# Splitting half of one 2 MB weight transfer by rows in a two-layer cached-attention decode

## The chip, the cores and the metric

The kernel runs on one core of a Trainium2 chip. The core has engines for computing (PE, the matrix engine; DVE, the vector engine; ACT, the scalar engine; POOL, GpSimd) and SP, SyncE, which here issues the transfers from HBM into the on-chip memory of 128 rows (SBUF). The transfers themselves are carried out by 16 DMA engines. The metric is device time in microseconds of one execution; lower is better.

## The reference

Two layers of the same pair of blocks, with the same weights and the same cache in both layers, run on one token for each of two sequences:

```python
x = x + A(layernorm(x), k_cache, v_cache, wq, wo)
x = x + B(layernorm(x), W_gate, W_up, W_down)
# and once more the same two lines
```

Block A is attention of one query position on a cache: 32 query heads of 128, in groups of 4 on 8 cached heads, 32768 cached positions, softmax over them, and the way out through `wo` (4096 x 512). Block B is a gated unit: `(gate * (gate > 0)) * up`, with `gate` and `up` of width 1792, and the way down to 512. All is float32. The cached keys and values are 8 x 2 x 32768 x 128 numbers each, 268 MB each in one layer's reading, so two layers read some 1.1 GB.

## The kernel before

**Tiling.** A pair of a cached head and a sequence is one turn; a layer has 16 turns (`NG`, L17). The keys of a turn are a matrix of 128 rows by 32768 numbers, and the values likewise. Each comes in two halves of 128 rows of 64 KB (8 MB), so a turn has four such transfers: first half of keys, second half of keys, first half of values, second half of values. They go into three buffers of 8 MB (`X`, `Z`, `Y`, L34) that are used in rotation. A transfer can start only when PE has finished with what the buffer held.

**A turn** (`lap`, L615 to L637) runs in this order: the second half of the values of the turn before (PE, into the accumulator `acc`); the keys' first half, among whose blocks the output of the turn before is multiplied with the way out's weights (`head_out`, `project`); the keys' second half; the softmax (DVE, ACT); the values' first half. Turns are a hardware loop on PE, DVE and ACT. SP isn't in the loop: its issues are written out one after the other, and it issues them in the order in which the program names the transfers. An issue that has to wait holds back all that stand behind it.

**The way out's weights.** `wo` is laid out as 128 rows; a cached head has 8 KB in each row (`WO`, L46). Two heads' shares lie side by side in a place of 16 KB a row (`WO_AT`). In layer 1 the heads run downward. At the end of each odd turn from turn 3 on either the next two heads' shares are loaded (`fetch_out`, L367, called at L635, in turns 3, 7 and 11), or POOL copies the second of them (`other`) to the place from which PE reads (`weights`), or, in the last turn, one head's share is loaded (L633). In layer 1 `weights` is the second 8 KB of a row and `other` the first. The next issue on SP after such a load is the second half of the same turn's values, at the start of the next turn; after it come the two halves of that next turn's keys. The first of these is given `(weights,)` as a further thing to wait for (L619), so that PE, which waits for the keys, needn't wait for the weights as well.

**Semaphores.** Each transfer has a lane, a semaphore that counts its completions. Transfers into the three buffers have a lane for each buffer; the loads of `wo` in the turns have the lane `wo`; all others go through 16 lanes in turn (`LANES`, L33; `fetch`, L353). A transfer on a lane waits for the one before it on the same lane.

**The end of layer 1** reads the last half of values in three pieces, then the gated unit's weights (`wgu`, three transfers, `UNITS`) and the way down (`wd`, six transfers, `DOWN`), all 128 rows high, and writes 64 KB out.

Of the kernel before, what the change touches and what calls it, by code (L numbers as in the profile page):

```python
# [11 lines left out]
P = 128  # L12
# [20 lines left out]
LANES = 16  # L33
# [11 lines left out]
P_AT, MT_AT, ACS_AT, WO_AT = FLOW, FLOW + 2 * D, FLOW + 2 * D + 32, FLOW + 3 * D + 32  # L45
WO = 4 * D  # L46
# [9 lines left out]

UNITS = (5, 3, 2, 1, 5, 2, 3, 4, 2, 3, 2), (16, 8, 8)
DOWN = (4, 3, 2, 4, 1), (4, 4, 2, 2, 1, 1)
QUERY = 4, 2, 3, 3, 1, 3, 2, 3, 2, 2, 3, 2, 2

C_SAME, C_SELH, C_PAIR, C_COL, C_HALF, C_MEAN, C_END = 0, 128, 144, 176, 178, 180, 181
# [247 lines left out]
def attention_reglu_decode(nc, hold, x, k, v, wq, wo, wgu, wd, out):  # L309
    tape = Tape(nc)  # L310
    pe, dve, act, pool, sp = map(tape.engine, ("tensor", "vector", "scalar", "gpsimd", "sync"))

    def sbuf(name, width):
        return hold.enter_context(nc.sbuf_tensor(name, [P, width], F32))[:, :]
# [4 lines left out]
    arena = sbuf("arena", ARENA)  # L319
# [9 lines left out]
    def tile(at, width):  # L329
        return arena[:, at : at + width]  # L330
# [8 lines left out]
    turn = [0, FLOW, 0, RING[0]]  # L339
# [8 lines left out]
    def ring(width):  # L348
        at = turn[1] if turn[1] + width <= RING[1] else turn[3]
        turn[1] = at + width  # L350
        return at

    def fetch(at, src, lane=None, also=()):  # L353
        t = arena[:, at : at + src.shape[-1]]
        if lane is None:
            lane = f"lane{turn[2] % LANES}"
            turn[2] += 1
        sp.dma_start(t, src, lane=lane, also=also)
        return t

    def half(src, n, h, at, also=()):
        return fetch(at, src[n, h], f"slot{at // ROW}", also)
# [4 lines left out]
    def fetch_out(h, n, t, lane="wo"):  # L367
        return fetch(t.offset, wo[:, h * WO : (h + n) * WO], lane)

    dve.memset(xq, 0.0)  # L370
    for b in range(NB):
        act.dma_start(bass.AP(xq.tensor, xq.offset + b * P, [[32 * P, 4], [1, P]]), x[:, b, :], lane=f"x{b}")
# [63 lines left out]
    def queries(L, total, first, between):  # L436
# [7 lines left out]
        else:  # L444
            begins = {sum(QUERY[:e]): n for e, n in enumerate(QUERY)}
        for e, b in enumerate(order):
# [29 lines left out]
    def place_queries(n, step=0):  # L476
        dve.tensor_copy(qz[:, 28 : 28 + REP], moving(lambda turn: bass.AP(
            qT.tensor, qT.offset + (1 + n) * REP + turn * (step * REP), [qT.ap[0], [1, REP]])))
# [8 lines left out]
    def soft_max(scores=scores):  # L487
        m1, nm, rs = own(0), own(1), own(2)
        dve.tensor_reduce(m1, scores, AX.XY, ALU.max)
        mt = tile(MT_AT, 32)  # L490
        dve.tensor_scalar_mul(mt, pair, m1)
        pe.matmul(small[0][:, :32], same, mt, start=True, stop=True)
        dve.tensor_reduce(nm, small[0][:, :32], AX.X, ALU.max, negate=True)
        act.activation(tile(P_AT, 2 * D), scores.rearrange("p a b -> p (a b)"), AF.Exp, bias=nm, scale=1.0, accum_out=rs)

    def soft_tail():
        pT, p = tile(PT_AT, 2 * D), tile(P_AT, 2 * D)
        for B in range(2):
            dve.transpose(pT[:, B * D : (B + 1) * D], p[:, B * D : (B + 1) * D])
        pe.matmul(small[1][:, 0:1], same, own(2), start=True, stop=True)  # L500
        dve.reciprocal(own(3), small[1][:, 0:1])
# [11 lines left out]
    def evacuate(split=True):  # L513
        acs = tile(PT_AT if split else ACS_AT, D)
        w = P if split else D
        for t in range(0, D, w):
            dve.tensor_scalar_mul(acs[:, t : t + w], acc[:, t : t + w], own(3))
        return acs

    def head_out(b, acs, weights=None):  # L520
        for t in range(4):
            pe.matmul(small[0][:, :REP], acs[:, t * P : (t + 1) * P], selh[:, 4 * t : 4 * t + 4], start=t == 0, stop=t == 3)
        if weights is not None:
            project(weights)
            dve.memset(oT, 0.0)
        dve.tensor_copy(moving(lambda turn: bass.AP(oT.tensor, oT.offset + (turn + b) % NB, [oT.ap[0], [NB, REP]])), small[0][:, :REP])
# [28 lines left out]
    def feed_forward(last, total):  # L555
# [25 lines left out]
        c = 0  # L581
        for n in DOWN[last]:
            t = fetch(Z + c * D if last else ring(n * D), wd[:, c * D : (c + n) * D])
# [11 lines left out]
    for L in range(NLAYER):  # L595
        last = L == NLAYER - 1
# [8 lines left out]
        def keys(h, t, first=0, scores=scores):  # L605
            for e in range(0, t.shape[-1] // D, 8):
                k_blocks(h + e, t[:, e * D : min(t.shape[-1], (e + 8) * D)], first, scores)
                yield e

        def values(lo, t, first=False, final=False):  # L610
            n = t.shape[-1] // D
            for e in range(0, n, 8):
                v_blocks(lo + e, lo + min(e + 8, n), t[:, e * D : min(e + 8, n) * D], first and e == 0, final and e + 8 >= n)

        def lap(i, second, k_first):  # L615

            values(HALF, second or half(v, seq[i - 1], 1, b), False, True)
            evacuate(False)
            for e in keys(0, k_first or half(k, seq[i], 0, a, (weights,) if i > L else ())):  # L619
                if e == 8:  # L620
                    head_out(1, tile(ACS_AT, D), weights)
            if not last and i == NG - 1:
                pool.tensor_copy(tile(RING[1], KEPT), tile(a, KEPT))
            for _ in keys(HALF, half(k, seq[i], 1, c)):
                pass
            soft_max()
            soft_tail()
            values(0, half(v, seq[i], 0, a), True)
            place_queries(seq[L] + step, step)
            if i % 2 == 1 and i > 1 and (last or i + 1 < NG):  # L630
                h = seq[i] // NB
                if h == 0:
                    fetch_out(h, 1, weights)  # L633
                elif i % 4 == 3:
                    fetch_out(h - last, 2, tile(WO_AT, 2 * WO))  # L635
                else:
                    pool.tensor_copy(weights, other)  # L637

# [7 lines left out]
        if last:  # L646
            n, e = divmod(KEPT, D)
# [28 lines left out]
        for i in tape.laps(range(L, NG), 1):  # L676
            lap(i, *ready.pop(i, (None, None)))
        nothing(op, False)
        combine()
        n = seq[NG - 1]  # L680
        for lo, hi in ENDING if last else FLOWN:
            t = fetch(b + lo * D, v[n, 1, :, lo * D : hi * D])
# [44 lines left out]
```

## Time and profile before

| | |
|---|---|
| time, median of 3 runs | 2556.66 us (2556.43 to 2556.95) |
| time of the profiled execution | 2556.44 us |
| its span, first to last instruction | 2555.0 us |
| PE busy | 1332.5 us (52%) |
| DVE, ACT, POOL busy | 156.9, 60.3, 18.2 us |
| read from HBM | 1102.99 MB, 432 GB/s over the span |

The page splits the span in 40 slices and gives for each the mean busy share of the 16 DMA engines and what they moved. Queues are told apart by number: q1 is the one that SP's transfers go through, q10 that of ACT's two small loads of x, and the queues of the kind "instruction" bring the program's code. A packet is one piece that a DMA engine moves; those of 4 bytes are completions. In the timeline an entry with SPq is the issue of a transfer, not the transfer. A wait at L212 is one of several waits ahead of an instruction, one at L214 the last, attached to the instruction itself.

### The profile page before, as it was taken

To read this page: it belongs to the slowest core of one execution; us is meant where nothing else is said; L and a number is where in the kernel's file an instruction comes from. 1 tells how busy PE (TensorE), PEld (TensorE's weight loads), DVE (VectorE), ACT (ScalarE), POOL (GpSimd) and SP (SyncE) were. 2 spreads that over 40 slices of the span, in tenths; PEclk is the share of its full clock that TensorE was granted. 3 is DMA by queue.
4 is the path that set the end of the run, shared out by engine and by line. 5 is a ranking of instruction groups with operands and counts; after the bars stand their busy time and mean duration, and the time that the engine had idled before them with its cause. 6 is when DMAs were issued, how large, how long until landed. Compare 5 with 4: busy or idle time off the path is not lost.

```text
span 2555.0 us, 20568 instructions
## 1 busy us (share of the span) xinstructions
PE 1332.5 (52%) x9542; PEld 364.7 (14%) x9542; DVE 156.9 (6%) x409; ACT 60.3 (2%) x82; POOL 18.2 (1%) x25
## 2 busy tenths in 40 slices
PE   4554545445444554455586554455445544454456
PEld 1111111111111111111121111111111111111112
DVE  1000000000000000000111000000000000000001
ACT  0000000000000000000000000000000000000000
POOL 0000000000000000000000000000000000000000
PEclk9777767777777777777798777777766777677778
DMA  9999999999999999999999999999999999999999
GB/s 425 429 440 427 428 442 430 440 429 434 434 430 440 430 433 434 430 440 430 424 422 440 431 439 429 434 434 433 437 429 435 434 433 436 429 437 432 434 435 391
DMA packets 26526, 1103.28 MB, mean 432 GB/s; under 512 B 2952, under 2 KB 3216, under 8 KB 6928
## 3 DMA queue, kind: packets, MB, share of 16 engines
q1 hardware_dynamic: 26496, 1103.06, 100.0%
q8 instruction: 12, 0.20, 0.0%
q14 instruction: 2, 0.02, 0.0%
q10 hardware_dynamic: 16, 0.00, 0.0%
HBM read 1102.99 MB, written 0.07 MB: 432 GB/s over the span
## 4 chain that ended last, share of the span: by engine, by line
DMA 73%; PE 26%; issue 0%; SPq 0%; DVE 0%; ACT 0%; ACTq 0%
DMA arena<-k 37%; DMA arena<-v 34%; PE acc L214 12%; PE pair L214 11%; DMA arena<-wd 1%; PE op L214 1%; PE small L214 1%; DMA arena<-wgu 1%; DMA arena<-wq 1%; SPq L214 0%; DVE pair L214 0%; DVE stat L214 0%; DVE arena L214 0%; DVE small L214 0%; DVE xq L214 0%
## 5 line engine op out<-in xcount | busy, mean ns | idle before, releaser
L214 PE MATMUL acc<-arena 128*16 128x512 f32 (+2 forms) x4288 | 616.3, 730 | 530.8 <-DMA arena<-v 521.5
L214 PE MATMUL pair<-arena,qz 128*32 128x512 f32 x4098 | 587.8, 727 | 558.9 <-DMA arena<-k 558.9
L214 PEld LDWEIGHTS pair<-arena,qz 128*32 128x32 f32 x4098 | 150.2, 131 | 987.1 <-issue 699.1
L214 PEld LDWEIGHTS acc<-arena 128*16 128x16 f32 (+1 forms) x4288 | 137.7, 113 | 972.5 <-issue 603.1
L214 ACT ACTIVATE arena<-pair,stat 128x1024 f32<-128x1024 f32 x32 | 35.6, 1113 | 2386.9 <-DVE stat L214 2386.9
L214 DVE TENSOR_SCALAR arena<-acc,stat 128x512 f32<-128x512 f32 (+1 forms) x39 | 25.5, 667 | 1052.1 <-PE acc L214 1052.1
L214 DVE TENSOR_REDUCE stat<-pair 128x1 f32<-128x1024 f32 x32 | 39.2, 1224 | 633.9 <-PE pair L214 633.9
L214 DVE STREAM_TRANSPOSE arena<-arena 128x512 f32<-128x512 f32 (+1 forms) x68 | 43.4, 674 | 40.8 <-ACT arena L214 40.7
L214 PE MATMUL small<-stat,cst 128*128 128x1 f32 (+1 forms) x72 | 16.2, 295 | 48.6 <-ACT arena L214 48.6
L214 PE MATMUL small<-arena,cst 128*128 128x32 f32 x64 | 13.1, 286 | 51.6 <-DVE arena L214 51.6
L214 PEld LDWEIGHTS small<-cst,arena 128*128 128x128 f32 x264 | 32.1, 191 | 28.9 <-issue 27.2
L214 PE MATMUL small<-cst,arena 128*128 128x4 f32 x264 | 35.0, 256 | 0.5 <-DVE arena L214 0.5
L214 PE MATMUL op<-arena,oT 128*2 128x512 f32 (+1 forms) x312 | 34.4, 526 | 0.4 <-DVE oT L214 0.3
L214 DVE MEMSET oT<- 128x8 f32 x33 | 2.1, 65 | 511.7 <-PE op L214 511.7
L214 POOL COPY arena<-arena 128x2048 f32<-128x2048 f32 (+1 forms) x7 | 13.4, 1921 | 2191.4 <-PE op L214 2045.7
L214 PE MATMUL op<-arena 128*32 128x448 f32 (+1 forms) x128 | 20.0, 572 | 5.6 <-DMA arena<-wq 3.1
L214 PEld LDWEIGHTS small<-stat,cst 128*128 128x128 f32 x72 | 13.2, 229 | 56.9 <-ACT arena L214 52.2
L214 PEld LDWEIGHTS small<-arena,cst 128*128 128x128 f32 x64 | 9.5, 188 | 80.5 <-DVE arena L214 80.5
L214 ACT ACT_TABLE_LOAD x16 | 20.5, 1283 | 11.4 <-DMA xq<-x 11.2
L214 PE MATMUL acc<-cst 128*32 128x448 f32 (+1 forms) x48 | 18.3, 479 | 0.0
L214 PE MATMUL small<-cst,stat 128*128 128x2 f32 x8 | 1.7, 287 | 18.7 <-DVE stat L214 18.1
L214 PE MATMUL small<-arena 128*32 128x128 f32 x224 | 8.8, 277 | 3.0 <-DMA arena<-wd 2.3
(63 smaller groups left out, 98.8 us busy)
## 6 DMA issues: line engine op xcount, KB each, us to landing
arena<-wo SPq DMA_DIRECT2D x6, 2048.0 KB, 32.0
arena<-v SPq DMA_DIRECT2D x2, 4096.0 KB, 37.8
arena<-wo SPq DMA_DIRECT2D x4, 1024.0 KB, 26.0
arena<-wd SPq DMA_DIRECT2D x4, 1024.0 KB, 23.4
arena<-wq SPq DMA_DIRECT2D x5, 768.0 KB, 6.3
arena<-wgu SPq DMA_DIRECT2D x1, 3584.0 KB, 44.1
arena<-wgu SPq DMA_DIRECT2D x2, 1792.0 KB, 48.4
arena<-v SPq DMA_DIRECT2D x2, 1536.0 KB, 40.9
```

Source lines behind the costliest of these rows:

```text
L214: ins = getattr(engine, op.call)(*args, **op.kw)
```

## The change

In turn 7 of layer 1 the load of two heads' shares (128 rows of 16 KB) is replaced by seven transfers. The first has all 128 rows of the first 8 KB (`other`). The second 8 KB (`weights`) come as six transfers of rows 0, 1, 2 to 3, 4 to 7, 8 to 31 and 32 to 127. All seven use the 16 lanes in turn rather than the lane `wo`. All other loads stay.

```diff
+FEW = (0, 1), (1, 2), (2, 4), (4, 8), (8, 32), (32, P)
...
+    def fetch_few(h, n, t):
+        fetch(t.offset, wo[:, h * WO : (h + n - 1) * WO])
+        for lo, hi in FEW:
+            at = t.offset + (n - 1) * WO
+            sp.dma_start(arena[lo:hi, at : at + WO], wo[lo:hi, (h + n - 1) * WO : (h + n) * WO], lane=f"lane{turn[2] % LANES}")
+            turn[2] += 1
...
-                    fetch_out(h - last, 2, tile(WO_AT, 2 * WO))
+                    (fetch_few if last and i == 7 else fetch_out)(h - last, 2, tile(WO_AT, 2 * WO))
```

## The prediction

> **What bounds the kernel now.** I read the page first (its transfers, its queues, the chain), then the stretches around the place of the change, the sync queue's waits there, and last the transfers' own view of the final 4 us.
>
> ```profile
> span 2555.0 us, 20568 instructions
> DMA packets 26526, 1103.28 MB, mean 432 GB/s; under 512 B 2952, under 2 KB 3216, under 8 KB 6928
> q1 hardware_dynamic: 26496, 1103.06, 100.0%
> q8 instruction: 12, 0.20, 0.0%
> q10 hardware_dynamic: 16, 0.00, 0.0%
> DMA 73%; PE 26%; issue 0%; SPq 0%; DVE 0%; ACT 0%; ACTq 0%
> ```
>
> SyncE's queue q1 fills 100.0% of the time of the 16 DMA engines. The chain gives 26% to PE, but that is a matter of how it hops: a landing, the matmuls that it frees, the buffer that they free, the next issue. It doesn't mean that the engines of the transfers rest meanwhile. The stretches of one turn in layer 1 say the same:
>
> ```profile
> core 0: us, PE busy (x) PEld busy (x) DVE busy (x) ACT busy (x) POOL busy (x), PEclk, DMA share, GB/s
> 1849.00:1887.00 38.00, 20.46 (x132) 5.36 (x132) 3.08 (x7) 1.21 (x2) 0.00 (x0) 0.69 1.01 435
> 1887.00:1912.00 25.00, 9.89 (x64) 2.03 (x64) 0.75 (x1) 0.00 (x0) 0.00 (x0) 0.66 1.00 435
> ```
>
> PE works 20.46 of 38 us, the transfers all of it. So the bytes are the bound: at 435 GB/s over 16 engines one engine moves 27.2 GB/s, and a row of 8 KB takes 8192 / 27.2 = 0.30 us of **one** engine. With every engine busy from start to end, the end is that of the engine with the most work. How unequal are they? The share of busy engines in the last 4 us shows it, in 40 slices of 0.1 us from 2548.5:
>
> ```profile
> DMA  9997999999989977747934333333322121100000
> q8 instruction: 1, 0.02, 1.7%
> ```
>
> The same stretch by half microseconds, and the last rows of PE and DVE:
>
> ```profile
> 2550.00:2550.50 0.50, 0.50 (x12) 0.22 (x14) 0.00 (x0) 0.00 (x0) 0.00 (x0) 1.00 0.80 291
> 2550.50:2551.00 0.50, 0.50 (x12) 0.47 (x11) 0.00 (x0) 0.00 (x0) 0.00 (x0) 1.00 0.37 143
> 2551.00:2551.50 0.50, 0.50 (x11) 0.22 (x12) 0.00 (x0) 0.00 (x0) 0.00 (x0) 1.00 0.30 115
> 2551.50:2552.00 0.50, 0.50 (x21) 0.42 (x17) 0.00 (x0) 0.00 (x0) 0.00 (x0) 1.00 0.18 70
> 2552.56 0.16 PEld L214 LDWEIGHTS small<-arena 128*32 128x32 f32 x8 [0.32 <-DMA arena<-wd]
> 2553.05 0.29 DVE L214 TENSOR_TENSOR xq<-xq,small 128x128 f32<-128x128 f32 x1 [5.31 <-PE small L214]
> ```
>
> The first engines run out at about 2550, a third of them (0.30 of 16, about five) works on to 2551.5, and two or three until nearly 2552.0. PE's last matmuls wait for that (0.32 us, releaser wd). Were all engines even, the last would end earlier by the mean idle share: 0.5 x (0.20 + 0.63 + 0.70 + 0.82) = 1.2 us. **No shift of rows between engines can bring more than that.** One source of the inequality stands in the second line above: the instruction queue took 1.7% of 16 x 4 us, that is 1.1 us, for one block, and there are 12 blocks on the page. A block that goes through one engine makes that engine 1.1 us late.
>
> **The change part by part.** *What goes.* One transfer of 128 rows of 16 KB; each engine has 8 of its rows. That eight holds comes from the packets:
>
> ```profile
> L214 SPq DMA_DIRECT2D arena<-v x68: 327/429/447, 56.4 to 2478.4; - x68
> L214 SPq DMA_DIRECT2D arena<-k x66: 327/328/1303, 1.7 to 2436.8; - x66
> L214 SPq DMA_DIRECT2D arena<-wq x14: 327/328/432, 0.8 to 1322.3; - x14
> L214 SPq DMA_DIRECT2D arena<-wgu x14: 327/328/741, 1271.4 to 2493.6; - x14
> L214 SPq DMA_DIRECT2D arena<-wd x11: 327/328/5982, 1294.4 to 2521.7; - x11
> L214 SPq DMA_DIRECT2D arena<-wo x10: 327/432/434, 1.2 to 2476.9; - x10
> L214 SPq DMA_DIRECT2D out<-xq x1: 348/348/348, 2553.4 to 2553.4; - x1
> xq<-x ACTq DMA_DIRECT2D x2, 2.0 KB
> ```
>
> The counts add to 184 issues, and 26496 / 184 = 144 packets: 128 rows and 16 completions, one for each engine. The two transfers of x have four rows each and make the 16 packets of q10, so four rows and four completions apiece: **a transfer of few rows uses no more engines than it has rows.**
>
> *What comes.* The first half, 128 rows of 8 KB, is spread evenly as before. Of the second half the one-row transfers use one engine each, then two, then four; 24 rows in equal shares can be 2 on each of 12 engines or 3 on each of 8; 96 rows are 6 on each of 16. If the small ones all begin at the same engine, that one now has 1+1+1+1+2+6 = 12 rows (13 with shares of three) where it had 8, a second one 10, two more 9, and those that only the 96 reach have 6. So a single engine's work moves by -2 to +4 rows (+5 at the outside): **-0.6 us to +1.2 us (+1.5)**. The sum of the bytes is as before. Whether the four x engines are the first four, and whether the same engine always starts, no view says, and the views don't name engines.
>
> [...]
>
> *Fixed cost of six transfers more.* The nearest rows are those of layer 0's weights, transfers of 448 KB and up, close together: a stretch of them and its packets.
>
> ```profile
> 1278.00:1296.00 18.00, 14.00 (x121) 5.37 (x116) 2.71 (x14) 0.63 (x1) 0.56 (x1) 1.00 1.02 419
> DMA packets 1506, 7.54 MB, mean 419 GB/s; under 512 B 160, under 2 KB 288, under 8 KB 1137
> ```
>
> The 160 packets under 512 B are the completions of ten transfers. At 419 for 435 GB/s the 18 us hold 18 x 0.037 = 0.66 us of loss, 0.07 us a transfer if all of it is put down to them. The first engine gets all six that are new, so it pays 6 x 0.07 = 0.4 us at most; at least, 0. I take 0.1, since the share of 1.02 shows no engine at rest in between.
>
> *Issue and waits.*
>
> ```profile
> 1848.10 0.33 SPq L214 DMA_DIRECT2D arena<-v  x1
> 1848.47 0.43 SPq L214 DMA_DIRECT2D arena<-wo  x1
> 1848.95 0.43 SPq L214 DMA_DIRECT2D arena<-v  x1
> 1885.96 0.80 SPq L214 DMA_DIRECT2D arena<-k  x2
> SPq L212 <- DMA arena<-wo: 31.2, 1, 31.2
> SPq L214 <- PE acc L214: 5.3, 1, 5.3
> L212 SPq EVENT_SEMAPHORE  x16: 17/17/17, 321.5 to 2323.2; - x16
> 1899.99 9.89 PE L214 MATMUL acc<-arena 128*16 128x512 f32 x64 [14.09 <-DMA arena<-v]
> ```
>
> Six issues more at 0.43 plus 0.05 delay the second v by 2.9 us, to about 1851.8. Its cover: the wo ahead of it in the queue lands only at 1849.4 + 31.2 = 1880.6, so the engines reach it 29 us after it is issued. Cost nothing. The next k issue waits for the weights and then, 5.3 us longer, for PE to leave the buffer; behind it on SyncE stands only the other half of k. The one wait becomes six, five more of 17 ns. Landing up to 1.5 us later still fits into the 5.3 us. If that cover were gone, a second one stands behind it: the v before k lands at 1899.99, 14 us after the issue. Lateness costs only from about 19 us on. The other reader, GpSimd's copy, wants the first half and comes two turns later.
>
> *The sum.* Whatever an engine gets ahead or behind in this turn it keeps: every later transfer is even over the engines and none runs dry. So the end moves by what happens to the engines that are last at 2552.0, or by the first engine if it becomes the last. With engines unnamed, the nearest reading is that the two or three late ones are among those whose rows stay (eight of 16 keep 8 rows) and that the first engine, early or in the middle, stays under the late ones: 0 + 0.1 us. The profiled execution took 2556.44 us, 1.4 more than its span, and lies 0.2 under the median of 2556.66: 2556.44 + 0.1 = 2556.54; with the median it would be 2556.76. I say **2556.6**.
>
> **The rivals.** *The late engines lose rows.* If all late ones are among the four with 6 rows, they end 0.6 us earlier, and the last matmuls with them, by 0.3 (the wait of that row) to 0.6: 2555.8 to 2556.1. For it: lateness is there to be removed, 2.0 us from first to last. Against it: two or three must sit in one group of four, and one that doesn't keeps the end.
>
> *The first engine becomes the last.* Its place is the end of the final wd transfer, its price up to +1.2 us (+1.5 with shares of three), and up to 0.4 for its completions; it decides from where that engine stands now less than 1.2 us ahead of the last one. At 2550.8, 1.2 us before the end, the share is between 0.37 and 0.30, some five of 16 engines, so about one chance in three: 2557.0 to 2558.1. This is the other side.
>
> *The small transfers go one at a time.* If each had to land before the next begins, the other engines would rest.
>
> ```profile
> out<-xq SPq DMA_DIRECT2D x1, 64.0 KB, 1.5
> ```
>
> A small transfer on an empty queue needs 1.5 us from issue to landing; five of that kind (the 96 rows are the sixth and fill all engines) are 7.5 us: 2563.9. It decides if the engines without a share in a small transfer don't go on to the v behind it. Against it: ten transfers in 18 us with share 1.02, where this would leave gaps. [...]
>
> *The change doesn't spread as it says.* If a one-row transfer were cut over all engines, the shift shrinks to the few-row transfers' 2 rows or less: 2556.4 to 2556.9. The x transfers' one packet a row speak against it.
>
> **How the numbers follow.** Forecast 42%, late engines relieved 24%, first engine last 28%, one at a time 3%, not spread 3%. A measurement of this kernel can tell about 0.2% from no change, 5.1 us; only the one-at-a-time case passes that, and I leave 1% for a gain and 1% for a loss from causes that I don't see. So faster 0.01, same 0.95, slower 0.04. The range takes in the relieved case with the runs' own spread (2556.43 to 2556.95) and nearly all of the first-engine case: 2555.7 to 2558.1. One further block of instructions that falls on a late engine (1.1 us) lies within it.
>
> **What would show it.** In the changed kernel: 190 issues on SyncE, and 26496 + 164 = 26660 packets on q1 if 24 rows use 12 engines (256 rows and 52 completions in place of 144 packets); the stretch 1849 to 1912 at share 1.00 still; SyncE's wait on PE before the k of that turn shorter than 5.3 by no more than 1.5 us; the slope of the last 2 us changed in form (one engine alone at the end would be the first-engine case; a steeper end the relieved one). The prediction is wrong if the engines' share falls in that turn, if k is issued later than 1885.96 by more than 1 us against the turns around it, or if the end moves by over 1.5 us.

## The result and the profile after

| | before | changed |
|---|---|---|
| median of 18 runs each, taken together | 2556.58 us (2556.39 to 2558.42) | 2561.00 us (2559.95 to 2562.70) |
| profiled execution, its span | 2556.44, 2555.0 us | 2561.30, 2560.1 us |

The changed kernel is 4.4 us slower, a ratio of 1.0017 (95% interval 1.0009 to 1.0024). The predicted 2556.6 us and its range up to 2558.1 missed that: the time lies above the range, and the sign of the difference is clear, though it is under the 0.2% that the prediction took for the limit of what can be told.

First the changed kernel's page: span, packets and the queue of SyncE.

```profile
span 2560.1 us, 20577 instructions
DMA packets 26691, 1103.29 MB, mean 431 GB/s; under 512 B 2988, under 2 KB 3252, under 8 KB 6964
q1 hardware_dynamic: 26660, 1103.06, 99.9%
```

The 26660 packets are the number worked out ahead, and 2988 - 2952 = 36 further completions are those of 1 + 1 + 2 + 4 + 12 + 16 engines. So the sum fits the numbers of engines that the prediction supposed; which ones, a count doesn't say. The queue is as full as before (99.9 and 100.0%). Now the issues of SyncE and its waits in turn 7 (the waits' columns are: total us, times, longest us), and PE's rows that wait for a landing.

```profile
1848.55 0.33 SPq L215 DMA_DIRECT2D arena<-v  x1
1848.92 2.41 SPq L215 DMA_DIRECT2D arena<-wo  x7
1851.37 0.43 SPq L215 DMA_DIRECT2D arena<-v  x1
1886.79 0.82 SPq L215 DMA_DIRECT2D arena<-k  x2
```

```profile
SPq L213 <- DMA arena<-wo: 34.2, 3, 27.0
SPq L215 <- PE acc L215: 0.7, 1, 0.7
```

```profile
1856.93 9.48 PE L215 MATMUL pair<-arena,qz 128*32 128x512 f32 x64 [8.44 <-DMA arena<-k]
1877.14 9.60 PE L215 MATMUL acc<-arena 128*16 128x512 f32 x64 [6.58 <-DMA arena<-v]
1905.18 9.23 PE L215 MATMUL acc<-arena 128*16 128x512 f32 x64 [18.45 <-DMA arena<-v]
```

The same rows of PE before, of which the prediction showed the third:

```profile
1856.47 9.48 PE L214 MATMUL pair<-arena,qz 128*32 128x512 f32 x64 [8.43 <-DMA arena<-k]
1875.92 9.98 PE L214 MATMUL acc<-arena 128*16 128x512 f32 x64 [5.81 <-DMA arena<-v]
```

From the start of the first row to the start of the third is a **stretch** that all runs below are measured by: 1899.99 - 1856.47 = 43.52 us before, 1905.18 - 1856.93 = 48.25 us after. The difference, **4.73 us**, is the whole loss; the first row is 0.46 us later already (5.1 us of span in all). The values behind the weights land later, though they were issued at 1851.37 and no engine was at rest (q1 99.6% from 1848 to 1901 us). That shows in the stretches of 10 us in which the weights are moved (the last two columns are the share of busy engines and GB/s), before and after:

```profile
1876.00:1886.00 10.00, 9.90 (x64) 2.18 (x63) 0.00 (x0) 0.00 (x0) 0.00 (x0) 0.71 1.14 492
1886.00:1896.00 10.00, 0.00 (x0) 0.00 (x0) 0.00 (x0) 0.00 (x0) 0.00 (x0) 0.63 1.00 433
```

```profile
1876.00:1886.00 10.00, 8.86 (x60) 2.26 (x64) 0.00 (x0) 0.00 (x0) 0.00 (x0) 0.69 1.08 315
1886.00:1896.00 10.00, 0.73 (x8) 0.00 (x0) 0.00 (x0) 0.00 (x0) 0.00 (x0) 0.66 1.00 433
```

The share stays at 1 or above (a packet counts where it starts, so 10 us can hold more than 10), but the bytes fall from 492 to 315 GB/s (over the longer stretch from 1848 to 1901 us, where such edges weigh less, from 435 to 399): **the engines are busy (share 1.08) and slow**. The packet records of the trace, which have start, duration and size, say how slow. This table was made from them for the packets that start in turn 7:

```
              pieces of the weights, median      summed over all,    v pieces over 2.45 us:
                                                 divided by 16       count, excess / 16
before        128 of 16 KB: 0.611 us             4.89 us             0
changed       first 96 of 8 KB: 0.309 us         7.44 us             24, 1.24 us
              the other 160, by 32: 0.51 to 0.61 us
```

A piece of 8 KB that took 0.309 us takes 0.51 to 0.61 us in the median once the small transfers run, and 24 pieces of the values beside and behind them take up to 4.48 us in place of 2.42. That is (7.44 - 4.89) + 1.24 = 3.8 us for the average engine. The remaining 0.9 us are put down to the distance between the engines, which was larger at the end (changed kernel, windows of 0.5 us):

```profile
2553.50:2554.00 0.50, 0.27 (x5) 0.09 (x8) 0.00 (x0) 0.00 (x0) 0.00 (x0) 1.00 0.88 340
2554.00:2554.50 0.50, 0.50 (x23) 0.50 (x26) 0.00 (x0) 0.00 (x0) 0.00 (x0) 1.00 0.52 201
2554.50:2555.00 0.50, 0.50 (x21) 0.42 (x12) 0.00 (x0) 0.00 (x0) 0.00 (x0) 1.00 0.22 86
2555.00:2555.50 0.50, 0.50 (x8) 0.15 (x7) 0.00 (x0) 0.00 (x0) 0.00 (x0) 1.00 0.35 111
2555.50:2556.00 0.50, 0.50 (x14) 0.43 (x10) 0.00 (x0) 0.00 (x0) 0.00 (x0) 1.00 0.11 41
2556.00:2556.50 0.50, 0.50 (x10) 0.26 (x12) 0.00 (x0) 0.00 (x0) 0.00 (x0) 1.00 0.06 25
2556.50:2557.00 0.50, 0.50 (x18) 0.43 (x12) 0.00 (x0) 0.00 (x0) 0.00 (x0) 1.00 0.06 25
```

0.06 is one engine of 16: it works on alone for a microsecond where before two or three shared the end. Summed as in the prediction, the average engine is done 0.5 x (0.12 + 0.48 + 0.78 + 0.65 + 0.89 + 0.94 + 0.94) = 2.4 us before the last one, where it was 1.2. Whether that last engine is the one with 12 rows isn't shown, since the records don't name engines; two equal halves, below, leave as large a rest.

### The profile page after: what moved, and what is told of

The parts are those of the page before. It is cut to its first block, busy times and chain, and to the rows that moved or that the text cites. A ratio compares the mean times of both kernels' runs of the same rounds, so it can differ in the third digit from the quotient of the medians.

```text
span 2560.1 us, 20577 instructions
## 1 busy us (share of the span) xinstructions
PE 1325.1 (52%) x9542; PEld 363.2 (14%) x9542; DVE 156.9 (6%) x409; ACT 60.3 (2%) x82; POOL 18.1 (1%) x25
## 2 busy tenths in 40 slices
DMA packets 26691, 1103.29 MB, mean 431 GB/s; under 512 B 2988, under 2 KB 3252, under 8 KB 6964
## 3 DMA queue, kind: packets, MB, share of 16 engines
q1 hardware_dynamic: 26660, 1103.06, 99.9%
## 4 chain that ended last, share of the span: by engine, by line
DMA 73%; PE 26%; issue 0%; SPq 0%; DVE 0%; ACT 0%; ACTq 0%
DMA arena<-k 37%; DMA arena<-v 34%; PE acc L215 12%; PE pair L215 11%; DMA arena<-wd 2%; PE small L215 1%; PE op L215 1%; DMA arena<-wq 1%; SPq L215 0%; DMA arena<-wgu 0%; DVE stat L215 0%; DVE arena L215 0%; DVE xq L215 0%; ACT arena L215 0%; ACTq L296 0%
## 5 line engine op out<-in xcount | busy, mean ns | idle before, releaser
L215 PE MATMUL acc<-arena 128*16 128x512 f32 (+2 forms) x4288 | 607.9, 722 | 541.9 <-DMA arena<-v 531.0
```

What stands on the lines that cost most here:

```text
L215: ins = getattr(engine, op.call)(*args, **op.kw)
```

## The experiments

The theories: **P**, the place that is written: a transfer that leaves out rows makes several engines write into the same part of the memory. **I**, the unequal loads (12 rows on one engine). **C**, a fixed cost of each transfer. **H**, the rows that are read. All kernels touch only the load in turn 7 of layer 1. The stretch is read as above, from one profiled execution each; the kernels without a loss lie between 43.5 and 43.7 us.

| run | second half of the load | stretch | median, before of the same call | ratio (95%) |
|---|---|---|---|---|
| e1_columns | six column pieces of all rows | 43.66 us | 2556.99, 2556.68 | 1.0002 (0.9992 to 1.0011) |
| e2_halves | rows 0-63, 64-127 | 49.53 | 2562.34, 2556.68 | 1.0020 (1.0011 to 1.0030) |
| e5_32_96 | rows 0-31, 32-127 | 48.07 | 2561.32, 2556.63 | 1.0019 (1.0010 to 1.0029) |
| e8_halves_wgu | as e2, read elsewhere | 48.83 | 2562.03, 2556.63 | 1.0020 (1.0010 to 1.0029) |
| e9_source | all rows, read as in e2 | 43.59 | 2557.02, 2556.63 | 1.0002 (0.9992 to 1.0011) |
| e10_every_other | even rows, odd rows, with a wait | 46.25 | 2561.26, 2556.63 | 1.0018 (1.0008 to 1.0027) |
| e11_every_other_free | the same without the wait | 43.57 | 2557.03, 2556.66 | 1.0002 (0.9992 to 1.0011) |
| e12_every_other_half | even and odd rows of each half | 49.53 | 2561.55, 2556.60 | 1.0020 (1.0010 to 1.0029) |
| e3_rows_own, e4_rows_other | unchanged, and 8 rows more | 50.40, 48.55 | 2563.43 and 2562.75, 2556.68 | 1.0025, 1.0022 |
| e6_rows_own, e7_rows_other | unchanged, and 8 short rows more | 43.54, 43.61 | 2556.62 and 2556.74, 2556.66 | 1.0000, 1.0000 |

### Number of transfers, or rows left out

```diff
-FEW = (0, 1), (1, 2), (2, 4), (4, 8), (8, 32), (32, P)
+FEW = (0, 256), (256, 512), (512, 768), (768, 1024), (1024, 1536), (1536, 2048)
...
-            sp.dma_start(arena[lo:hi, at : at + WO], wo[lo:hi, (h + n - 1) * WO : (h + n) * WO], lane=f"lane{turn[2] % LANES}")
+            fetch(at + lo, wo[:, u + lo : u + hi])
```

> As many transfers as in the change (seven), but the second half is cut by columns: six pieces of all 128 rows, 1, 1, 1, 1, 2 and 2 KB wide. The measure is the stretch from the start of the second keys' matmuls of turn 7 to the start of the matmuls that wait for the values behind the weights: 43.52 us before, 48.25 us in the changed kernel. Theory P (a transfer that leaves out rows makes several engines write into the same part of the memory, and they slow each other): all rows are there, so 43.5 to 43.9 us and a time within 0.5 us of before. Theory I (only the unequal loads, 12 rows on one engine): the loads are equal, 43.5 us. Theory C (each transfer has a fixed cost that the engines can't hide): as many transfers, so about 47 to 48 us and a time 3 to 4.5 us over before.

```diff
-FEW = (0, 1), (1, 2), (2, 4), (4, 8), (8, 32), (32, P)
+FEW = (0, 64), (64, P)
```

> The second half comes as two transfers of 64 rows, 0 to 63 and 64 to 127: four rows on each of 16 engines in each, equal loads. Theory P: if 64 rows reach only half of the places, each transfer takes twice its 1.2 us, so the stretch of 43.52 us grows by about 2.4 us to 45.9, and the time by about 2.4 us. Theory I: equal loads, 43.5 us and no change. Theory C: two transfers more where the change has six, so a third of its 4.7 us: 45.1 us.

The window of 10 us of the column pieces, then that of the halves with the rows of PE that begin and end the stretch:

```profile
1876.00:1886.00 10.00, 9.04 (x64) 2.01 (x56) 0.00 (x0) 0.00 (x0) 0.00 (x0) 0.79 1.12 466
```

```profile
1876.00:1886.00 10.00, 8.47 (x64) 2.07 (x64) 0.00 (x0) 0.00 (x0) 0.00 (x0) 0.81 1.15 290
...
1857.51 9.66 PE L215 MATMUL pair<-arena,qz 128*32 128x512 f32 x64 [8.25 <-DMA arena<-k]
...
1907.04 8.78 PE L215 MATMUL acc<-arena 128*16 128x512 f32 x64 [21.63 <-DMA arena<-v]
```

Seven transfers of all rows in place of one cost 0.14 us, so C falls, and with it the rival of transfers that go one at a time. Two transfers of 64 rows, equal on all engines if the rows are given out evenly (no record names an engine), cost **6.0 us, more than the change's six**: theory I can hardly be the main part. P holds in kind, but it had been given 2.4 us. The packet records show the rest: the 8 KB pieces sum to 7.73 us an engine in place of 4.89, about what was expected, and the pieces of the values behind add 2.0 us: by theory P, an engine that has gone on to the values meets one that is still writing weights in its place. That makes 4.8 of the 6.0 us; the other 1.2 are left over although each transfer has 64 rows for 16 engines.

### Without the small transfers

```diff
+FEW = (0, 32), (32, P)
```

> The change without its small transfers: the second half as rows 0 to 31 and 32 to 127, two and six rows on each of 16 engines, equal loads. [...] Theory I (one engine's extra rows): no engine has any, 43.5 us. If the one-row pieces are the cost: 43.5 to 44 us.

The stretch is 48.07 us, 4.55 over before. The change's transfers of 1, 1, 2, 4 and 24 rows together are thus worth 0.2 us more than one of 32 by the stretch, and nothing more by the medians (2561.00 and 2561.32 us): the cut by contiguous rows costs, not the small transfers.

### Read or written

```diff
-            sp.dma_start(arena[lo:hi, at : at + WO], wo[lo:hi, (h + n - 1) * WO : (h + n) * WO], lane=f"lane{turn[2] % LANES}")
+            sp.dma_start(arena[lo:hi, at : at + WO], wgu[lo:hi, 0:WO], lane=f"lane{turn[2] % LANES}")
```

> The two halves of 64 rows again, but read from the gated unit's weights (rows 14 KB apart in HBM in place of 64 KB), so the weights hold numbers that don't belong there. Theory P (the place that is written): as with the halves of wo, stretch 49 to 50 us and a time of 5 to 6.5 us over before. Theory H (the rows that are read lie badly in HBM): another distance, so another loss, nearest none: 43.5 to 45 us.

```diff
+        for e in range(2):
+            fetch(at + e * WO // 2, bass.AP(wo.tensor, wo.offset + e * 64 * row, [[row // 2, P], [1, WO // 2]]))
```

> Only the reading is as in the halves: two transfers of all 128 rows of the buffer, 4 KB each, the first reading two pieces of each of the rows 0 to 63 of wo, the second of the rows 64 to 127; the weights get numbers of other rows and columns. Theory P: all rows are written, so 43.5 to 43.9 us and a time within 0.6 us of before. Theory H: as with the halves, 49 to 50 us and 5 to 6.5 us over before.

Reading other rows, 14 KB apart, leaves the loss (48.83 us). Reading only rows 0 to 63 and then only 64 to 127, but writing all rows (in pieces of 4 KB), has none (43.59 us). H falls: the loss follows the rows that are written.

### Alternating rows

```diff
+        for e in range(2):
+            sp.dma_start(arena[e:P:2, at : at + WO], wo[e:P:2, u : u + WO], lane=f"lane{turn[2] % LANES}")
```

> Two transfers of 64 rows again, but rows 0, 2, 4, ... and then 1, 3, 5, ..., the same on both sides. [...] Theory H: half of the rows of wo at twice the distance, a loss like the halves' (49 us) or another. A loss that comes from 64-row transfers as such, wherever the rows are: 49.5 us.

This run told nothing by its time. The kernel's planner of waits keeps rows as a range from first to last, so the odd rows' transfer overlapped the even rows' and waited for their landing. SyncE's timeline and waits show it:

```profile
1849.64 30.45 SPq L215 DMA_DIRECT2D arena<-wo  x3
1880.13 0.59 SPq L215 DMA_DIRECT2D arena<-v  x1
```

```profile
SPq L215 <- DMA arena<-wo: 28.9, 1, 28.9
```

The values behind were issued at 1880.13 rather than about 1850, and by that order the queue ran dry. Of the 64 pieces of the odd rows 21 took 0.32 to 1.14 us in place of 0.31. That need not be a collision: they started from rest, and from rest the very first 16 pieces of 64 KB in the kernel before, of a transfer of all 128 rows, took 2.74 to 3.43 us in place of 2.42. With a mark that keeps the two transfers from being ordered:

```diff
-                    if engine != "tensor" or other.token[0] != engine:
+                    if (engine != "tensor" or other.token[0] != engine) and not (apart and other.apart == apart):
```

> The alternating rows once more, now without the wait of the second transfer for the landing of the first: in the run before this the planner took their rows for overlapping, the queue ran dry and all engines came together. Theory P (contiguous rows reach too few places; alternating ones reach all): 43.5 to 44 us of stretch, a time within 0.6 us of before, the engines as far apart behind the transfers as ahead of them. Theory T (any transfer of 64 rows collides when another follows at once): the halves' 6.0 us, 49.5 us.

```diff
-        for e in range(2):
-            sp.dma_start(arena[e:P:2, at : at + WO], ...
+        for lo, hi in (0, 64), (1, 64), (64, P), (65, P):
+            sp.dma_start(arena[lo:hi:2, at : at + WO], ...
```

> Alternating rows within a half: four transfers of 32 rows (0, 2, ... 62; 1, 3, ... 63; 64, 66, ... 126; 65, 67, ... 127), two rows on each of 16 engines, without waits among them. It tells apart why alternating rows cost nothing. [...] Theory A (rows that aren't neighbours never collide, wherever they lie): 43.5 to 44 us and a time within 0.6 us of before.

The windows of the two, alternating rows of all 128 first, alternating rows of a half second, and for each the rows of PE that begin and end the stretch:

```profile
1876.00:1886.00 10.00, 8.78 (x64) 2.14 (x64) 0.00 (x0) 0.00 (x0) 0.00 (x0) 0.81 1.10 474
...
1856.90 9.98 PE L215 MATMUL pair<-arena,qz 128*32 128x512 f32 x64 [7.94 <-DMA arena<-k]
...
1900.47 8.66 PE L215 MATMUL acc<-arena 128*16 128x512 f32 x64 [15.35 <-DMA arena<-v]
```

```profile
1876.00:1886.00 10.00, 8.86 (x64) 2.20 (x64) 0.00 (x0) 0.00 (x0) 0.00 (x0) 0.73 1.11 276
...
1857.22 8.93 PE L215 MATMUL pair<-arena,qz 128*32 128x512 f32 x64 [7.28 <-DMA arena<-k]
...
1906.75 9.75 PE L215 MATMUL acc<-arena 128*16 128x512 f32 x64 [20.42 <-DMA arena<-v]
```

This is the decisive pair. 64 alternating rows over the whole memory cost nothing that can be told (474 GB/s, 43.57 us; all 256 pieces of 8 KB take 0.309 to 0.316 us). Alternating rows inside a half cost as much as the contiguous halves (276 GB/s, 49.53 us). In these runs neither the number of rows (64 are free here and slow as halves) nor their being neighbours decides, but whether the transfer's rows are spread over the whole memory or lie in a part of it. One difference is left in the pair: inside the halves the transfers have 32 rows, not 64, and 32 rows spread over the whole memory weren't tried.

That speaks for theory P, the place that is written, by which the loss here is that of the contiguous halves. How many parts the memory has isn't shown. The transfer of rows 32 to 127 ran only together with that of rows 0 to 31 (48.07 us), so neither of the two has a figure of its own.

### Eight single rows, two sets of them

```diff
+    def fetch_more(h, n, t):
+        fetch_out(h, n, t)
+        for r in MORE:
+            sp.dma_start(arena[r : r + 1, RING[1] : RING[1] + WO], wo[r : r + 1, h * WO : (h + 1) * WO], lane=f"lane{turn[2] % LANES}")
```

> The kernel before, and in turn 7 of layer 1 behind the 2 MB load eight further transfers of one row of 8 KB each: rows 0 to 3 and 32 to 35, into a place that nothing reads afterwards. That is 64 KB more work. If all run on one engine it gets 8 x 0.31 = 2.5 us more. [...] Theory C: eight transfers more, 6 us for all engines. The stretch grows by at most 2.5 us, less what the engine stood ahead of the last one (0.3 to 2.3 us), and one engine alone runs at the end.

> As the run with rows 0 to 3 and 32 to 35, but with rows 64 to 67 and 96 to 99, also into a place that nothing reads. [...] Theory C: as with those rows.

The question is whether eight rows cost more when they are 64 to 67 and 96 to 99 than when they are 0 to 3 and 32 to 35. Neither run answers it. The columns were not free: they overlap 1376 of the weights' 2048, so eight rows of the weights were written over with other columns, and each transfer waited for the load itself. SyncE's timeline of the run with rows 0 to 3 and 32 to 35:

```profile
1850.30 33.64 SPq L215 DMA_DIRECT2D arena<-wo  x9
1883.98 0.36 SPq L215 DMA_DIRECT2D arena<-v  x1
```

The values were issued 34 us late, and the 6 to 7 us are those of a dry queue (from 1876 to 1886 us a share of 0.67, 256 GB/s). A second pair uses 896 free columns (3.5 KB a row); the second part of the diff makes the last transfer of the kernel wait for them:

```diff
+            sp.dma_start(arena[r : r + 1, OWN - 896 : OWN], wo[r : r + 1, h * WO : h * WO + 896], lane=f"lane{turn[2] % LANES}")
...
-    sp.dma_start(out, xq, lane="out")
+    sp.dma_start(out, xq, lane="out", also=(tile(OWN - 896, 896),))
```

> The kernel before, and behind the 2 MB load of turn 7 eight transfers of one row of 3.5 KB (rows 0 to 3 and 32 to 35) into columns that nothing else uses in this layer, so nothing waits for them. One row takes 0.14 us of one engine by the 3.5 KB pieces elsewhere in the trace. Theory P: one engine is 8 x 0.14 = 1.1 us later, no other engine is touched: the stretch grows by 0 to 1.1 us, depending on where that engine stood (it was 0.3 to 2.3 us ahead of the last).

> The same with rows 64 to 67 and 96 to 99. Theory P: these rows lie in a place that another engine is writing all the time with 64 KB pieces, so the one-row pieces take about twice as long and that other engine is delayed as well: two engines 1 to 2.2 us later where the run with rows 0 to 3 and 32 to 35 has one, the stretch longer by 0 to 2.2 us. If places don't matter: one engine, 1.1 us, as there.

The packet records of the eight rows in ns, in order, and of the 64 KB pieces that started while they ran or as the last one ended:

```
rows 0-3, 32-35     140 140 140 140 140 140 140 140     no piece over 2440
rows 64-67, 96-99   140 140 140 140 187 278 278 278     one of 3382, one of 2728
```

Rows 0 to 3 and 32 to 35 go at 140 ns, and no other piece is slowed. Rows 64 to 67 and 96 to 99 go at 140 ns at first; from 0.1 us after a piece of the values has begun they go at up to 278 ns, and that piece takes 3.38 us in place of 2.42. The two kernels differ only in the rows. **These rows and the piece beside them slow each other**: the rows take up to 278 ns in place of 140, and the piece is 0.96 us late. That two engines then write in the same place is what theory P says; the records name neither engines nor places. The time shows nothing of it (2556.62 and 2556.74 us against 2556.66), so the engines that were held up were presumably not near the last (an estimate from the records: 0.96 us later for the piece's engine, 1.58 us for one that has all eight rows).

## Why the prediction was wrong

- *The bytes are the bound, and the end is that of the most loaded engine.* Right. The loss in turn 7 is kept to the end: 0.46 us ahead of the stretch and 4.73 in it make up the 5.1 us of the span, with the queue at 99.9%. At the very end one engine's share is left, 0.06.
- *A row of 8 KB takes 0.30 us of one engine; the sum of the bytes is as before.* **This is the step that failed.** The 0.30 us come from transfers of all 128 rows, whose pieces keep that time beside each other (0.309 us beside the column pieces). In the cut transfers the pieces take 0.51 to 0.61 us in the median, and 24 pieces of the values beside and behind them up to 4.48 us in place of 2.42: 3.8 us on the average engine, where the prediction had 0. The other runs show where: the loss came with rows that lie in a part of the memory (halves 49.53 us, rows 0 to 31 and 32 to 127 48.07), and not with transfers that write all over it (column pieces 43.66, alternating rows 43.57). From this step came the bounds of -0.6 to +1.5 us, and so the range.
- *One engine with 12 rows, four with 6, eight that keep 8.* This was the author's estimate, and the forecast's 0 for the late engines rests on it. No run shows which engine has which rows, nor that the small transfers begin at the same one; the counts (26660 packets, 36 further completions) fit 12 engines for the 24 rows. What the runs showed in place of that 0 is the loss of the pieces above. One engine does work on alone at the end, as in the rival given 28%, but that is 0.9 of the 4.7 us at most, and 12 rows aren't shown to be the reason: the halves, of 64 rows each, leave a rest of 1.2 us too, and the run with 32 and 96 rows lost 4.55 in all.
- *Six more transfers cost 0.1 us.* Right as far as can be told: 0.14 us of stretch with six column pieces, small pieces included.
- *The waits of SyncE.* Right that they cost nothing, wrong in size: the wait on PE shrank from 5.3 to 0.7 us, not by at most 1.5, because the weights landed late. The values were issued at 1851.37, where 1851.8 was worked out; seven issues took 2.41 us.
- *Transfers that go one at a time, 3%.* Falls with the column pieces, and with the eight one-row transfers of 3.5 KB, which cost nothing that the time shows. It was the only case with a time above the range, and its 7.5 us had the right side for the wrong reason.
- *What would show it.* "Share 1.00 still" was no test: the share was about 1 in the kernels with the loss and without it. GB/s in the same window told them apart, 492 and 315.
- *A measurement tells about 0.2%, 5.1 us.* The interval from 1.0009 to 1.0024 tells less than that, 0.17% from none. That the time stayed under 5.1 us was luck: the loss came from none of the terms.

No run was faster than before by more than the measurement tells. The loads could be evened by 1.2 us at most, as worked out ahead.

**Open:** the trace doesn't record which engine writes which row. How the rows of an alternating transfer are given out isn't shown either; in the run without the wait no piece of them was slowed (0.309 to 0.316 us). What sets the last 0.9 us, the distance between the engines, is open as well.

## What to carry to other kernels

Where transfers are the bound, as here (q1 at 100.0%), compare a cut by rows with one by columns. Here six pieces by columns, all 128 rows in each, cost 0.14 us of the stretch, and alternating rows over the whole memory 0.05 us; two contiguous halves cost 6.0 us. Read GB/s beside the busy share: at shares of 1.14 and 1.08 the queue moved 492 and 315 GB/s, two thirds. A price per row was no constant: 0.309 us for 8 KB in transfers of all 128 rows, 0.51 to 0.61 us in the median in the cut ones.

## What the runs showed of the hardware

- Pieces of transfers with part of the rows took up to about twice as long in the median: 8 KB took 0.51 to 0.61 us in the changed kernel in place of 0.309. Single rows of 3.5 KB took up to 0.278 us as rows 64 to 67 and 96 to 99 (e7_rows_other), and 0.14 us as rows 0 to 3 and 32 to 35 (e6_rows_own). That two engines write the same part then is inferred from which rows are slow.
- The loss reaches the transfer behind: its pieces of 64 KB took up to 4.48 us (change) and 5.31 us (halves) in place of 2.42. That is 1.2 and 2.0 us on the average engine. It fits engines that are out of step, so that early ones meet late ones in their places; the records don't show this directly.
- Of 1 MB by halves of 64 rows the excess is 4.8 us on the average engine: 2.8 us in the weights' own pieces (7.73 in place of 4.89 us) and 2.0 us in those of the values behind.
